# Batch 1 in a fused attention and MoE kernel: v pooled on GpSimd, weight sums on VectorE, scores in two groups, half of q transposed later

## The chip, the core and the metric

The kernel runs on one core of a Trainium2 chip. Its engines are named as the profile names them: PE (TensorE, matrix products), ACT (ScalarE, functions of one input), DVE (VectorE), POOL (GpSimd) and SP (which only issues transfers here). Each engine works through its own list of instructions in order; a wait in the list holds up all that stands behind it on that engine. The metric is the time of one execution on the device in microseconds, as the median of three runs.

## The reference

Two stages. The first is attention over pooled keys: for each of 8 batches and 8 heads, k and v (576 rows of 64) are averaged over groups of 8 rows, which leaves 72 pooled rows; then

```python
scores = scale * np.matmul(q, k_p.transpose(0, 1, 3, 2))
attn = np.exp(scores - max)          # per row
attn = attn / np.sum(attn)           # per row
attn_out = np.matmul(attn, v_p)      # 576 x 64 per head
```

The second is a network over the 4608 x 512 matrix x that the heads make side by side: `h = x @ w_in` (512 to 2048), `g = h * cos(h)`, `out = g @ w_out` (2048 to 512). The output is float32.

## The kernel before

The 4608 rows of x are worked in nine tiles of 512 rows (t = 0 to 8). For each tile there is an *up* stage (x times w_in in eight blocks, `up_mm`, line 353; then cos on ACT, line 363, and the product on DVE, line 367, into `g_sb`) and a *down* stage. Attention of batch t + 1 is done beside tile t, and since a batch has 576 rows and a tile 512, 64 rows of batch t (called REST) are left for tile t's down stage. All matrix work is in bfloat16. The order on each engine is that in which the program is written (a manual schedule): what is written earlier stands earlier in the engine's list.

Tile 0 is different from the others. Its down stage is a plain product: 64 matmuls with a 512-wide right side (`down_mm`, line 370), numbered n = 0 to 63. They run in two halves of 32; within a half the four parts of w_out are taken in the order 0, 2, 1, 3, four matmuls for each of two row blocks. A list called `fill` says before which n other work is put: batch 1's `scores`, the pooling of its v, and its `values`. From tile 1 on the down stage uses seven half-size products instead of eight, which needs sums and differences of the parts of w_out (`put_weights`, line 387: for each of two halves i four arrays w1, w3, w2, w4, in this order of dependence) and of g (`put_g`, line 397). The eight weight arrays are made once, in tile 0.

For a group of heads and columns `scores` is a matrix product into a bank of PSUM (line 233) and an exponential on ACT (line 240) that writes `ex` to SBUF. `values` is a product of `ex` with pooled v (line 268), then logarithm and exponential on ACT for the inverse of the row sum (lines 274 and 275), then two products on DVE into `xT` (line 279). For batch 1 the groups are four, `us[0]` to `us[3]`: two column ranges of 256 for heads 0 to 3, then the same for heads 4 to 7. Heads 0 to 3 need the first half of the transposed q, heads 4 to 7 the second. There are three PSUM banks of double size (`banks`) and two single ones (`obanks`); the up stage of tile 0 uses the three in turn, and the down stage its obanks.

Pooling is done in one of two ways. Batches 0 and 1 are pooled by PE, as a product with a matrix of ones and zeros (`pool_k_mm`, line 177; `pool_v_mm`, line 185, with a copy to `vz` on DVE, line 187). Batches 2 and up are loaded in a layout with one pooled row per partition, and POOL adds the eight rows in three steps (`pool_first`, line 156, four instructions; `pool_rest`, line 162, two, then line 165 for k or 168 for v).

q is transposed by PE for batches 0 and 1 (`q_transpose_mm`, line 214, in 18 blocks of 128, with copies out of PSUM at line 215) and by transfers for the others. All input loads are issued by POOL in the order of the program, and share one queue; the issue of a load waits until the load eight before it has landed. `kv_st` has two buffers, one for each of two batches or for k and v of one.

What is in the loads' order ahead of tile 0: w_in parts, batch 1's k, the two halves of its q, w_out part 0, batch 1's v, w_out parts 2, 1, 3. After tile 0 in the program, and so behind on POOL, stand the loads of batch 2 and four of the weight sums, and then the pooling of batch 2.

Of the kernel before, what the change touches and what calls it, by code (L numbers as in the profile page):

```python
# [12 lines left out]
ADD = mybir.AluOpType.add  # L13
SUB = mybir.AluOpType.subtract

POOL = 8
# [4 lines left out]
def kernel(  # L21
# [9 lines left out]
    nc = tc.nc  # L31
    B, H, S, D = q.shape
    Sp = S // POOL
# [61 lines left out]
    def load_even(dst, b, src, j0=0, j1=KCH):  # L95
        nc.gpsimd.dma_start(out=dst[:, j0:j1].rearrange("p j t d -> p j (t d)"), in_=even_view(src, b, j0, j1))

    def kv_tile():
        return kvst.tile([128, 2 * KCH * ROW * D], BF16, name="kv_st", tag="kv_st")
# [5 lines left out]
    def kv_even_tiles(b):  # L105
        st = kv_tile()
        staged["k", b], staged["v", b] = even_part(st, 0), even_part(st, 1)
# [1 line left out]
    def q_tile(b):  # L109
        staged["q", b] = qst.tile([128, KCH, ROW, D], BF16, name="q_b", tag="q_b")  # L110

    def load_kv(b, which, src):

        st = kv_tile()[:Sp, 0:H * POOL * D].rearrange("p (h t d) -> p h t d", h=H, t=POOL)
        nc.gpsimd.dma_start(out=st.rearrange("p h t d -> p h (t d)"),
                            in_=src[b].rearrange("h (p t) d -> p h (t d)", t=POOL))
        staged[which, b] = st

    def load_q(b):
        q_tile(b)  # L120
        load_even(staged["q", b], b, q)
# [6 lines left out]
    def load_w_out(cg):  # L128
        nc.gpsimd.dma_start(
            out=w_out_sb[cg],  # L130
            in_=moe_w_out[cg * 512:(cg + 1) * 512, :].rearrange("(f p) m -> p f m", p=128))
# [19 lines left out]

    def pool_first(b, which):

        x, s = staged.pop((which, b)), half_sums
        for h in range(0, H, 2):
            nc.gpsimd.tensor_tensor(out=s[:, h:h + 2], in0=x[:, h:h + 2, 0:4, :], in1=x[:, h:h + 2, 4:8, :], op=ADD)  # L156

    def pool_rest(b, which):

# [345 lines left out]
    half_pi = consts.tile([128, 1], FP32, name="half_pi")  # L505
    nc.vector.memset(half_pi, math.pi / 2.0)

    kv_even_tiles(1)
    q_tile(1)
    for cg in range(3):  # L510
        load_w_in(cg)
    load_even(staged["k", 1], 1, k)
    load_even(staged["q", 1], 1, q, 0, 2)
    load_w_in(3)
    load_even(staged["q", 1], 1, q, 2, 4)
    load_w_out(0)
    load_even(staged["v", 1], 1, v)
    nc.gpsimd.memset(vz[1], float(POOL))
    for i in range(2):
        nc.gpsimd.memset(ring[i], 0.0)  # L520
    for cg in (2, 1, 3):
        load_w_out(cg)

    def warm_up(n, bank):

# [35 lines left out]
    for t in range(NT):  # L561
        b = t + 1
        if t > 0:

            for fp in up_order(t)[0:2]:
                up_mm(t, fp, 0, 2)
        for n, fp in enumerate(up_order(t)):
            up_mm(t, fp, 2 if n < 2 else 0)
            between = ()
            if t == 0:  # L570
                if fp == 4:
                    puts = pool_k_mm(1, obanks[0], 0, 2), pool_k_mm(1, obanks[1], 2, 4)
                elif fp in (5, 6):
                    g0 = 9 * (fp - 5)
                    puts = q_transpose_mm(1, obanks[0], g0, g0 + 5), q_transpose_mm(1, obanks[1], g0 + 5, g0 + 9)
                if fp in (4, 5, 6):
                    puts[0](vec)
                    between = ((puts[1], act),)
            up_g(t, fp, between)
            if 0 < t and 3 <= n < 6:  # L580
                put_gs(*[(k, 0) for k in (((3,), (1,), ()) if t == 1 else ((1, 2), (3,), (4,)))[n - 3]])
            if 0 < t and b < B:
                if n == 0:
                    q_transpose(b)
                    k_transpose(b)
                elif n == 2:
                    pool_rest(b, "v")
                    if b + 1 < B:
                        nc.gpsimd.tensor_copy(out=gate, in_=kk[b % 2][0:1, H - 1, 0:1])
                        load_q(b + 1)  # L590
                        load_kv(b + 1, "v", v)
            if n == 2:
                while stores:
                    stores.pop(0)()
        mms = [(ms, fc) for ms in range(4) for fc in range(FFCH)]
        if t == 0:
            mms = [(ms, fc) for hm in range(2) for cg in (0, 2, 1, 3) for ms in range(2 * hm, 2 * hm + 2)
                   for fc in range(4 * cg, 4 * cg + 4)]


        def S_(n, bank):
            return lambda: scores(b, us[n], banks[bank])

        later = []

        def V_(n, bank, wait=None):
            return lambda: values(b, us[n], banks[bank], wait)

        fill = []
        if t < B:  # L610
            exp_tables()
            fill = [(1, lambda: scores(t, REST, banks[2])), (16, lambda: values(t, REST, banks[1]))]
        if t == 0:
            fill = [(2, fill[0][1]), (2, S_(0, 0)), (8, lambda: pool_v_mm(1, banks[1])),
                    (8, lambda: values(t, REST, banks[2])), (8, S_(1, 0)), (8, V_(0, 1)),
                    (18, S_(2, 2)), (21, V_(1, 0, later)), (26, S_(3, 1)), (32, lambda: later.pop()()),
                    (32, V_(2, 2)), (40, V_(3, 0))]
        if t == FIRST:
            early_inverses.clear()
        if t < FIRST:  # L620
            fi = 0
            for n, (ms, fc) in enumerate(mms):
                while fi < len(fill) and fill[fi][0] <= n:
                    fill[fi][1]()
                    fi += 1
                down_mm(obanks[ms % 2], ms, fc)
                if fc == FFCH - 1:
                    down_out(t, ms, obanks[ms % 2])
                if n == 4:
                    put_weights(0, nc.vector, (1,))  # L630
                elif n == 36:
                    put_weights(1, nc.vector, (3,))
            put_weights(1, nc.vector, (2, 4))
        else:
            products, reads = down_products(t)

            def product(i, j=0, k=2 * HF):
                for mm in products[i][j:k]:
                    mm()

            later = []

            u0, u1, u2, u3 = [(b, CHUNKS[i], banks[j]) for i, j in enumerate((2, 1, 0, 1))]
            ur = (t, REST, banks[2])

            def scores_of(*parts):
                for part in parts:
                    scores_mm(*part)
                for part in parts:
                    scores_exp(*part)  # L650

            def muls():
                while later:
                    later.pop(0)()

            steady, rest = b < B, t < B
            if rest:
                exp_tables()
            product(0)
            product(1, 0, 2)  # L660
            if steady:
                scores_of(u0, u1, u2)
            elif rest:
                scores_of(ur)
            product(1, 2)
            if t == 1:
                put_g(2, 0)
            put_gs((1, 1), (2, 1))
            reads[0]()
            if not steady:  # L670
                reads[1]()
            put_gs((3, 1), (4, 1))
            if steady:
                reads[1]()
                values_rows(*u0)
            if t == 1:
                put_g(4, 0)
            product(2)
            reads[2]()
            if steady:  # L680
                values_rows(*u1)
                values_rows(*u2)
            product(3)
            reads[3]()
            muls()
            product(4)
            reads[4]()
            muls()
            if steady:
                scores_of(ur, u3)  # L690
            product(5, 0, 4)
            if rest:
                values(*ur, later)
            product(5, 4, 12)
            muls()
            if steady:
                values_rows(*u3)
            product(5, 12)
            reads[5]()
            muls()  # L700
            product(6)
            reads[6]()
        if t < B:
            sin_tables()
        if b + 1 < B:
            if t == 0:
                load_kv(b + 1, "k", k)
                load_q(b + 1)
                load_kv(b + 1, "v", v)
                put_weights(0, nc.gpsimd, (3, 2, 4))  # L710
                put_weights(1, nc.gpsimd, (1,))
            else:

                nc.gpsimd.tensor_copy(out=gate, in_=g4[0:1, HF - 1, 0:1])  # L714
            pool_first(b + 1, "k")
            if t != 1 and b + 2 < B:
                load_kv(b + 2, "k", k)
            pool_rest(b + 1, "k")
            if t == 1:
                load_kv(b + 2, "k", k)  # L720
            pool_first(b + 1, "v")
# [28 lines left out]
```

The softmax here doesn't subtract the row's maximum and nothing guards it: scores larger than these inputs give would overflow.

## Time and profile before

| | |
|---|---|
| time | 286.22 us median of 3 (285.98 to 286.24) |
| span of the profiled run | 284.8 us |
| PE busy | 276.2 us |
| DVE busy | 215.3 us |
| ACT busy | 164.4 us |
| POOL busy | 143.4 us |
| clock of PE | full speed throughout |
| up stage of tile 0 | 17.35 to 33.59 us |
| down stage of tile 0 | 33.59 to 53.20 us |
| tile 1 | 53.20 to 83.0 us |

Times in views are in microseconds from the start of the span. In the timeline a line gives start, length, engine, line of the kernel, operation, output and inputs with their shapes, and in brackets how long the engine had been idle and who released it. In the chain a line gives start, length and what was being waited for or worked on, followed back from the last instruction. "PEld" is the loading of PE's stationary side, which overlaps its products. A share of busy time is an average over stages; what a change is worth in one stage is read from that stage.

### The profile page before, as it was taken

To read this page: it belongs to the slowest core of one execution; us is meant where nothing else is said; L and a number is where in the kernel's file an instruction comes from. 1 tells how busy PE (TensorE), PEld (TensorE's weight loads), DVE (VectorE), ACT (ScalarE), POOL (GpSimd) and SP (SyncE) were. 2 spreads that over 40 slices of the span, in tenths; PEclk is the share of its full clock that TensorE was granted. 3 is DMA by queue.
4 is the path that set the end of the run, shared out by engine and by line. 5 is a ranking of instruction groups with operands and counts; after the bars stand their busy time and mean duration, and the time that the engine had idled before them with its cause. 6 is when DMAs were issued, how large, how long until landed. Compare 5 with 4: busy or idle time off the path is not lost.

```text
span 284.8 us, 5857 instructions
## 1 busy us (share of the span) xinstructions
PE 276.2 (97%) x2360; PEld 176.4 (62%) x2360; DVE 215.3 (76%) x314; ACT 164.4 (58%) x193; POOL 143.4 (50%) x150
## 2 busy tenths in 40 slices
PE   7889999999999999999999999999999999999994
PEld 2545554446874587458745884588458844874583
DVE  5448757899957995699569956995699569856972
ACT  3787798367257735674567556655656555436600
POOL 8553069996599259924993499439900000000000
PEclk9999999999999999999999999999999999999999
DMA  7999999793939698998678969882670261015014
GB/s 154 202 206 207 207 205 216 118 199 54 145 48 161 124 221 135 138 166 169 104 135 152 186 90 160 146 172 57 119 153 3 55 128 40 0 24 126 2 37 111
DMA packets 57738, 36.12 MB, mean 127 GB/s; under 512 B 35441, under 2 KB 53361, under 8 KB 57713
## 3 DMA queue, kind: packets, MB, share of 16 engines
q0 software_dynamic: 19744, 18.07, 41.1%
q1 hardware_dynamic: 37328, 17.18, 30.0%
q10 hardware_dynamic: 640, 0.52, 0.8%
q8 instruction: 18, 0.29, 0.4%
q14 instruction: 8, 0.06, 0.1%
HBM read 36.70 MB, written 9.44 MB: 162 GB/s over the span
## 4 chain that ended last, share of the span: by engine, by line
PE 86%; DVE 6%; ACT 3%; DMA 2%; issue 1%; POOL 0%; DVEq 0%; POOLq 0%; ACTq 0%
PE bank L353 35%; PE obank L431 32%; PE obank L370 4%; PE obank L353 4%; PE bank L233 3%; DVE g_sb L367 3%; DMA q_b<-in_q_dram 2%; PE bank L295 2%; PE bank L431 2%; PE bank L268 1%; DVE w L387 1%; DVE g L397 1%; ACT cos L363 1%; ACT ex L240 1%; DVE vz L187 0%
## 5 line engine op out<-in xcount | busy, mean ns | idle before, releaser
L353 PE MATMUL bank<-xT,w_in_sb 128*128 128x512 bf16 x512 | 114.0, 379 | 0.2 <-DVE g_sb L367 0.2
L363 ACT ACTIVATE cos<-bank,half_pi 128x1024 f32<-128x1024 f32 x64 | 70.4, 1114 | 56.9 <-PE bank L353 55.0
L353 PEld LDWEIGHTS <-w_in_sb 128*128 128x128 bf16 x576 | 56.1, 98 | 66.2 <-issue 0.9
L367 DVE TENSOR_TENSOR g_sb<-bank,cos 128x1024 bf16<-128x1024 f32 x64 | 77.1, 1219 | 25.1 <-ACT cos L363 24.9
L156 POOL TENSOR_TENSOR half_sums<-kv_st 72x512 f32<-72x512 bf16 x48 | 54.7, 1165 | 0.6 <-issue 0.2
L240 ACT ACTIVATE ex<-bank 72x1024 bf16<-72x1024 f32 (+1 forms) x40 | 35.0, 929 | 34.0 <-PE bank L233 33.8
L431 PEld LDWEIGHTS <-g 128*128 128x128 bf16 x512 | 47.9, 98 | 6.1 <-issue 0.3
L431 PE MATMUL obank<-w,g 128*128 128x256 bf16 x368 | 42.7, 272 | 0.2 <-DVE p_sb L445 0.2
L431 PEld LDWEIGHTS <-g_sb 128*128 128x128 bf16 x384 | 36.8, 98 | 6.9 <-DVE g_sb L367 0.3
L162 POOL TENSOR_TENSOR half_sums<-half_sums 72x512 f32<-72x512 f32 x24 | 30.4, 1288 | 0.0
L431 PE MATMUL obank<-w_out_sb,g_sb 128*128 128x256 bf16 x240 | 28.9, 273 | 0.0
L397 DVE TENSOR_TENSOR g<-g_sb 128x1024 bf16<-128x1024 bf16 x32 | 23.3, 728 | 0.5
L714 POOL COPY gate<-g 1x1 bf16<-1x1 bf16 x5 | 0.9, 179 | 34.1 <-DVE g L397 34.1
L279 DVE TENSOR_TENSOR xT<-bank,inv 64x256 bf16<-64x256 f32 x14 | 5.9, 422 | 15.0 <-ACT inv L275 14.9
L300 DVE TENSOR_TENSOR x_rows<-bank,inv_rows 128x512 bf16<-128x512 f32 x24 | 16.6, 691 | 0.8
L431 PE MATMUL obank<-w_out_sb,g 128*128 128x256 bf16 x112 | 15.6, 273 | 0.0
L431 PE MATMUL obank<-w,g_sb 128*128 128x256 bf16 x128 | 15.3, 273 | 0.0
L370 PE MATMUL obank<-w_out_sb,g_sb 128*128 128x512 bf16 x64 | 15.2, 379 | 0.0
L353 PE MATMUL obank<-xT,w_in_sb 128*128 128x512 bf16 x64 | 15.1, 379 | 0.0
L233 PE MATMUL bank<-qT,kk 64*72 64x128 bf16 (+2 forms) x288 | 12.7, 221 | 0.1
L233 PEld LDWEIGHTS <-kk 64*72 64x72 bf16 x288 | 8.8, 110 | 5.3 <-issue 3.8
L331 ACT ACT_TABLE_LOAD x9 | 11.5, 1283 | 0.9 <-PEq L734 0.7
(103 smaller groups left out, 277.1 us busy)
## 6 DMA issues: line engine op xcount, KB each, us to landing
out_dram<-o_two SPq DMA_DIRECT2D x64, 128.0 KB, 2.4
kv_st<-in_v_dram POOLq DMA_DIRECT2D x8, 576.0 KB, 11.2
kv_st<-in_k_dram POOLq DMA_DIRECT2D x7, 576.0 KB, 8.5
q_b<-in_q_dram POOLq DMA_DIRECT2D x6, 576.0 KB, 7.5
w_in_sb<-in_moe_w_in_dram POOLq DMA_DIRECT2D x4, 512.0 KB, 13.5
w_out_sb<-in_moe_w_out_dram POOLq DMA_DIRECT2D x4, 512.0 KB, 18.2
q_b<-in_q_dram POOLq DMA_DIRECT2D x4, 288.0 KB, 12.4
g_sb<-in_k_dram SPq DMA_DIRECT2D x1, 576.0 KB, 3.6
```

The source lines that it names most:

```text
L156: nc.gpsimd.tensor_tensor(out=s[:, h:h + 2], in0=x[:, h:h + 2, 0:4, :], in1=x[:, h:h + 2, 4:8, :], op=ADD)
L162: add(out=s[:, h:h + 4, 0:2, :], in0=s[:, h:h + 4, 0:2, :], in1=s[:, h:h + 4, 2:4, :], op=ADD)
L233: nc.tensor.matmul(pair[:Sp, bank, c:c + n].rearrange("p (g n) -> p g n", n=64), lhsT=kk[b % 2][half[r], key_slot(b, h0 + i, r), 0:Sp], rh ...
L240: nc.scalar.activation(out=ex[:, 0:nh * n].rearrange("p (a n) -> p a n", a=2), in_=pair[:Sp, :, 0:nh * n // 2], func=ACTF.Exp, scale=scale ...
L300: nc.vector.tensor_tensor(out=x[0:n].rearrange("p (j a d) -> p j a d", j=KCH, a=2), in0=ps[0:n, :, 0:2 * (D + 2)].rearrange("p j (a w) -> ...
L331: nc.scalar.preload_act_table_set("natural_log_exp_and_others")
L353: nc.tensor.matmul(h[j] if h is obanks else h[:, j, :], lhsT=w_in_sb[fc // 4][:, ki, (fc % 4) * 128:(fc % 4 + 1) * 128], rhs=xT[:, ki, t * ...
L363: nc.scalar.activation(out=c, in_=ps, func=ACTF.Sin, bias=half_pi[:, :1])
L367: nc.vector.tensor_mul(out=o, in0=ps, in1=c)
L370: nc.tensor.matmul(o, lhsT=g_sb[:, fc, ms * 128:(ms + 1) * 128], rhs=w_out_sb[fc // 4][:, fc % 4, :], start=(fc == 0), stop=(fc == FFCH - 1))
L397: nc.vector.tensor_tensor(out=out[:, f0:f1], in0=x, in1=y, op=op)
L431: mms.append(lambda bank=bank, first=first, g=g, w=w, fc=fc, p=p: nc.tensor.matmul(bank[p], lhsT=g(fc, p), rhs=w(fc), start=(first and fc ...
```

## The change

Five edits, all for batch 1 and tile 0.

1. Batch 1's v is loaded in the layout with pooled rows on partitions, in two parts of four heads (one into the second half of batch 1's `kv_st`, one into `g1`, which isn't used until tile 1), and pooled by POOL ahead of tile 0. `pool_v_mm(1, ...)` goes. This is to take that product from PE.
2. The loads' order becomes: w_out 0, v, w_out 2, the second half of q, w_out 1, w_out 3, and batch 2's k and q are issued ahead of the pooling of v.
3. The four weight sums that POOL did are put on DVE: w1 of half 0 after the sixth up block, the others at n = 24 of the down stage.
4. The second half of batch 1's q is transposed at n = 15 of the down stage, with both copies on DVE, instead of in the up stage with one copy on ACT.
5. Scores are put in two groups, REST with `us[0]` and `us[1]` at n = 8, `us[2]` with `us[3]` at n = 16; values of the first three groups stand together at n = 24, and their products on DVE are put off to n = 32.

```diff
-    def load_kv(b, which, src):
-        st = kv_tile()[:Sp, 0:H * POOL * D].rearrange("p (h t d) -> p h t d", h=H, t=POOL)
-        nc.gpsimd.dma_start(out=st.rearrange("p h t d -> p h (t d)"),
-                            in_=src[b].rearrange("h (p t) d -> p h (t d)", t=POOL))
-        staged[which, b] = st
+    def load_kv(b, which, src, homes=None):
+        homes = homes or [kv_tile()]
+        n = H // len(homes)
+        staged[which, b] = []
+        for i, home in enumerate(homes):
+            st = home[:Sp, 0:n * POOL * D].rearrange("p (h t d) -> p h t d", h=n, t=POOL)
+            nc.gpsimd.dma_start(out=st.rearrange("p h t d -> p h (t d)"),
+                                in_=src[b, i * n:(i + 1) * n].rearrange("h (p t) d -> p h (t d)", t=POOL))
+            staged[which, b] += [st[:, h:h + 2] for h in range(0, n, 2)]
...
-    load_even(staged["q", 1], 1, q, 2, 4)
     load_w_out(0)
-    load_even(staged["v", 1], 1, v)
+    load_kv(1, "v", v, [st[:, KCH * ROW * D:], g1.rearrange("p f n -> p (f n)")])
     nc.gpsimd.memset(vz[1], float(POOL))
     for i in range(2):
         nc.gpsimd.memset(ring[i], 0.0)
-    for cg in (2, 1, 3):
+    load_w_out(2)
+    load_even(staged["q", 1], 1, q, 2, 4)
+    for cg in (1, 3):
         load_w_out(cg)
+    load_kv(2, "k", k)
+    load_q(2)
+    pool_first(1, "v")
+    pool_rest(1, "v")
...
-                elif fp in (5, 6):
-                    g0 = 9 * (fp - 5)
-                    puts = q_transpose_mm(1, obanks[0], g0, g0 + 5), q_transpose_mm(1, obanks[1], g0 + 5, g0 + 9)
+                elif fp == 5:
+                    puts = q_transpose_mm(1, obanks[0], 0, 5), q_transpose_mm(1, obanks[1], 5, 9)
...
+            if t == 0 and fp == 5:
+                put_weights(0, nc.vector, (1,))
...
+        def late_q():
+            for put in [q_transpose_mm(1, banks[0][:, i, :], g0, g1) for i, g0, g1 in ((0, 9, 14), (1, 14, 18))]:
+                put(vec)
...
-            fill = [(2, fill[0][1]), (2, S_(0, 0)), (8, lambda: pool_v_mm(1, banks[1])),
-                    (8, lambda: values(t, REST, banks[2])), (8, S_(1, 0)), (8, V_(0, 1)),
-                    (18, S_(2, 2)), (21, V_(1, 0, later)), (26, S_(3, 1)), (32, lambda: later.pop()()),
-                    (32, V_(2, 2)), (40, V_(3, 0))]
+            fill = [(8, lambda: scores_of((t, REST, banks[2]), (b, us[0], banks[0]), (b, us[1], banks[1]))),
+                    (11, lambda: values(t, REST, banks[2], later)), (15, late_q),
+                    (16, lambda: scores_of((b, us[2], banks[0]), (b, us[3], banks[1]))), (16, muls),
+                    (24, V_(0, 2, later)), (24, V_(1, 0, later)), (24, V_(2, 1, later)),
+                    (24, lambda: put_weights(0, nc.vector, (3, 2, 4))), (24, lambda: put_weights(1, nc.vector, (1,))),
+                    (32, muls), (44, V_(3, 2))]
...
-                if n == 4:
-                    put_weights(0, nc.vector, (1,))
-                elif n == 36:
+                if n == 36:
                     put_weights(1, nc.vector, (3,))
...
-                load_kv(b + 1, "k", k)
-                load_q(b + 1)
                 load_kv(b + 1, "v", v)
-                put_weights(0, nc.gpsimd, (3, 2, 4))
-                put_weights(1, nc.gpsimd, (1,))
```

`scores_of` and `muls`, which existed for the later tiles, are moved up so that tile 0 can use them.

## The prediction

> **What bounds the kernel now.** First the page: busy times, to see which engine could set the end. Then the busy time by stage, then inside the odd stages the chain and the timeline.
>
> ```profile
> PE 276.2 (97%) x2360; PEld 176.4 (62%) x2360; DVE 215.3 (76%) x314; ACT 164.4 (58%) x193; POOL 143.4 (50%) x150
> ```
>
> TensorE (PE) is busy 97% of the span. What doesn't shorten PE's work or its few waits can't pay. By stage (columns: stretch, length, then busy time and instructions of PE, PEld, DVE, ACT, POOL, then clock, DMA share, GB/s): the up and the down matmul of tile 0, all of tile 1, all of tile 2.
>
> ```profile
> 17.35:33.59 16.24, 16.24 (x156) 8.42 (x155) 11.64 (x15) 11.69 (x16) 5.40 (x8) 1.00 1.23 207
> 33.59:53.20 19.61, 19.32 (x131) 9.52 (x130) 12.05 (x18) 16.34 (x23) 15.03 (x10) 1.00 1.10 195
> 53.20:83.00 29.80, 29.34 (x258) 19.52 (x257) 26.94 (x36) 17.05 (x19) 24.48 (x24) 1.00 0.73 118
> 83.14:112.16 29.02, 29.00 (x257) 19.30 (x256) 23.17 (x35) 17.05 (x19) 19.94 (x21) 1.00 0.95 151
> ```
>
> Tile 2 is full of PE (29.00 of 29.02 us), and the later steady tiles are like it. Tile 1 has the same work and takes 0.8 us more. All edits lie before or in tile 0's down matmul, so only the first three rows can change. The chain in the down stage and at its end:
>
> ```profile
> 36.22 1.19 PE bank L185 x18
> ...
> 37.50 0.70 DVE vz L187
> 38.20 0.05 issue
> 38.24 0.61 PE bank L268 x4
> ...
> 53.40 0.69 DVE o_two L375
> 54.09 2.21 DVE w L387
> 56.30 0.02 issue
> 56.32 1.65 DVE w L387
> 57.97 1.15 DVE g_sb L367
> ```
>
> Two things to see. Batch 1's v is pooled by PE (1.19 us), and its first values wait for the copy out of PSUM. And from 53.40 on the chain runs on VectorE (DVE): two weight sums take 3.9 us and hold back the first cos products of tile 1. Why they take so long is in the timeline of POOL (GpSimd) and DVE:
>
> ```profile
> 36.08 0.68 DVE L387 TENSOR_TENSOR w<-w_out_sb 128x1024 bf16<-128x1024 bf16 x1
> 53.23 2.50 POOL L162 TENSOR_TENSOR half_sums<-half_sums 72x512 f32<-72x512 f32 x2
> 54.01 2.28 DVE L387 TENSOR_TENSOR w<-w,w_out_sb 128x1024 bf16<-128x1024 bf16 x1
> 55.81 2.34 POOL L165 TENSOR_TENSOR ring<-half_sums 72x512 bf16<-72x512 f32 x2
> 56.32 1.65 DVE L387 TENSOR_TENSOR w<-w_out_sb,w 128x1024 bf16<-128x1024 bf16 x1
> ```
>
> The same sum is 0.68 us with POOL at rest, and 2.28 and 1.65 us beside POOL's adds: the first ends just after L162's pair does (55.73).
>
> [...]
>
> **The change, part by part.**
>
> *v pooled on POOL.* Removed from PE: 18 matmuls, 1.17 us of pure path, and DVE's copy (0.69 us) with the wait behind it. Added on POOL: four first adds of 1.15, two of 1.25, one of 1.27 us = 8.4 us, in place of the four weight sums there (4 x 2.13 = 8.5 us). What matters is when it ends. Landing times before, as issue plus time to landing: w_in's last part 27.8, q second half 29.3, w_out 0 31.8, v 34.7, w_out 2 37.2, w_out 1 40.0, w_out 3 42.4, k of batch 2 46.5 us; all in one queue at some 206 GB/s. In the new order w_out 0 lands at 30.4 (2.55 us a part), the two halves of v at 31.9 and 33.4 (1.45 each), w_out 2 at 36.0, q at 37.4; then w_out 1, w_out 3 and k as before, since the bytes ahead of them are the same. POOL then pools v from 32 to about 40.7 us. The first values stand at down matmul 24, which PE reaches at about 41.8: hidden, with 1 us to spare.
>
> *The second half of q's transposes moved into the down matmul.* Nine transposes, 0.50 us by the chain, leave the up stage and come back in the down stage: no change in work. What is new is a wait. They stand at matmul 15, their two copies are both on DVE (0.49 and 0.41 us), and only one down matmul (0.22 us) stands between them and the scores that read the result and reuse that bank. From the end of the transposes to the end of the second copy is about 0.9 us, so PE waits 0.7 us. Behind it on PE is everything; this is the largest new cost. Bounds: 0.4 if the first copy overlaps the transposes fully, 1.0 if DVE is late.
>
> *Scores in two groups.* The first group stands at matmul 8 and needs all three banks, the last being free only when the last cos product is done (ACT ends 1.3 us after the up stage, DVE 1.25 later): at about 35.7 us, where PE would be there at 35.4. Wait: 0.3 us. In exchange the old waits go: the stage of before holds 64 down matmuls (24 of them take 5.20 us on the chain, so 64 x 0.217 = 13.9), pooling 1.2, 16 scores in fours at 0.34 (1.4), 16 values in fours at 0.44 (1.8), the small ones of batch 0 some 0.4: 18.6 of 19.61 us, so 1.0 us was waiting or switching (the v copy, and values that waited for a bank, 0.53 us before 47.57 among them). In the new order ACT has an exponential per group done before PE asks for it: values of groups 0 to 2 stand together at 24, with the exponentials done at about 41.9 and w_out 3 landed at 42.4.
>
> *Weight sums on DVE.* One at 31.7 in the gap left by a q copy (w_out 0 landed at 30.4, so no wait in front of the cos product behind it). Four more at about 40.3 to 43.1, 0.69 each, when POOL has just finished pooling and waits for k (46.5): no blocking, and they end before the first output copy at 44.2. If v were late they would meet POOL's adds and cost 1.6 to 2.3 us each; then the output copies, and PE's second half behind them, come 1 to 4 us later. That is the upper bound of this edit.
>
> *Sum up to tile 1.* Up stage 16.24 - 0.5 = 15.7. Down stage: work 18.6 - 1.2 + 0.5 = 17.9; waits 0.7 (q), 0.3 (banks), 0 to 0.3 (w_out 2 at matmul 8, wanted at 36.0 and landing at 36.0), 0.1 (output copy): 19.0 to 19.3. Together 34.7 to 35.0 against 35.85: PE reaches tile 1 some 0.8 to 1.1 us earlier.
>
> *Tile 1.* Its start hangs on DVE's last two weight sums, which will again meet POOL. POOL pools k of batch 2 as soon as it lands, 46.5 instead of 47.14 (where it was held by its own weight sums): L162 and L165 come 0.65 us earlier. DVE arrives at the sums at about 53.5, in the middle of L162 again, and leaves 0.65 to 0.9 us earlier than 57.97. The gain that survives is the smaller: 0.65 to 0.9; I take 0.8.
>
> Forecast: 286.2 - 0.8 = 285.4 us.
>
> **The rivals.**
>
> *A: the new waits eat the gain.* The loads are just in time: w_out 2 and q are wanted within 0.5 us of landing. If v in its new shape (72 partitions) moves as slowly as k of batch 2 did (42.4 to 46.5, 4.1 us instead of 2.9), all behind it is 1.2 us later, PE waits that long at matmul 8, and 0.8 - 1.2 makes 286.6; with part of it, 286.2. Against: stores began at 45.3, in that same stretch, and the bandwidth stayed at 206 GB/s, so k wasn't slow but shared.
>
> *B: DVE becomes the bound; slower.* Pooling of v ends late (43 or after), the four weight sums run into it and take 1.7 us each, +4 us on DVE, half of it absorbed before the second half of the down matmul: 286.2 + 1.2 = 287.4. For: DVE is already the chain at the tile's border. Against: POOL has about 8 us between v's landing and the time that it is wanted, and little else to do.
>
> *C: more is won.* If DVE's last two sums fall beside POOL's work rather than into it (0.7 each instead of 2.2 and 1.65), tile 1 loses its 0.8 us too: 285.4 - 1.0 = 284.4. Against: k's landing, which starts POOL's adds, doesn't move.
>
> **How the numbers follow.** Forecast 55%, A 22%, B 13%, C 10%. The forecast's own bounds are 285.0 (all waits at their lower ends) to 285.8 (0.4 us more wait on w_out 2); the range takes in C's 284.4 and A's upper end, 286.8, and leaves out B. Faster by over 0.2% means under 285.65: most of the forecast (48 of 55) and C: 0.58. Within 0.2% (285.65 to 286.79): the rest of the forecast and most of A (18 of 22): 0.25. Slower: B and the end of A: 0.17.
>
> **What the profile of the changed kernel would show.** Right: no pooling of v on PE; PE's wait before the second group of scores, 0.7 us, released by DVE's q copies; vz written by POOL before 41.8 us; the four weight sums at 0.7 us each; the last two still at 1.6 to 2.3 beside L162 and L165; tile 1 begun by PE at about 52.3 instead of 53.2, and from tile 2 on 28.95 us a tile. Wrong: down matmuls waiting for a w_out part or for q's load (A), weight sums of 1.6 us or more near 41 us or output copies released late (B), or tile 1 down at 29.0 us (C). The prediction fails most easily on the load order, since every load there is wanted within a microsecond of landing.

## The result, and the profile after

The changed kernel takes 295.5 us (median of 4 runs, 295.02 to 298.52) against 286.23 us before in the same comparison (4 runs, 285.98 to 286.74): 1.034 times as long, with a 95% interval of 1.028 to 1.040. Forecast were 285.4 us, and a range up to 286.8. The prediction is wrong in sign, and off by 10 us.

In the changed kernel nearly every line number is 3 higher than before: the weight sums are L390, `put_g` is L400, POOL's first adds are L159, the next L165, the last L168 (k) and L171 (v), down matmuls L373, the products of later tiles L434. First the page of the changed kernel: busy times, and the clock granted to PE in 40 slices of 7.3 us.

```profile
PE 277.1 (94%) x2342; PEld 176.9 (60%) x2342; DVE 222.8 (76%) x318; ACT 164.0 (56%) x192; POOL 143.5 (49%) x154
...
PEclk9999999999959999999999999999999999999998
```

PE has no more to do than before (277.1 to 276.2 us), but 3 points less of the span: the time is idle time. DVE gained 7.5 us. And one slice of the clock stands out, the twelfth, from 81 to 88 us. The same stretches as in the prediction say where (length, then busy time of PE, PEld, DVE, ACT, POOL, then clock, DMA share, GB/s):

```profile
17.35:33.59 16.24, 16.24 (x149) 8.14 (x148) 11.75 (x15) 11.54 (x15) 7.59 (x11) 1.00 1.24 206
33.59:53.20 19.61, 16.99 (x117) 8.88 (x115) 12.80 (x20) 15.87 (x23) 12.55 (x12) 1.00 1.16 198
53.20:83.00 29.80, 24.07 (x183) 14.55 (x182) 29.24 (x30) 13.08 (x13) 24.70 (x24) 0.96 0.70 108
83.14:112.16 29.02, 28.76 (x235) 18.32 (x234) 21.40 (x32) 17.03 (x19) 11.87 (x14) 0.93 0.81 137
```

The up stage of tile 0 is as full as before. In the down stage's stretch PE idles 2.6 us (before 0.3), in tile 1's stretch 5.7 (before 0.5). DVE is busy 29.24 of 29.80 us there (before 26.94), which looks like more work; 6.39 us of it are one blocked instruction, as the timeline below shows. By PE's first matmul of each stage, tile 0 takes 36.7 us (before 35.8), tile 1 37.7 (before 29.8), and all that follows 0.4 us more than before; PE began 0.3 us earlier. Together 0.9 + 7.9 + 0.4 - 0.3 = 8.9 us; the profiled spans differ by 8.8. PE's waits between 17 and 95 us (total, times, longest):

```profile
PE obank L434 <- DVE v_sb L450: 5.4, 1, 5.4
PE obank L373 <- DMA w_out_sb<-in_moe_w_out_dram: 1.6, 2, 0.8
PE bank L236 <- DVE qT L218: 0.8, 1, 0.8
```

The first is the large loss. The timeline of the changed kernel about it:

```profile
72.98 1.91 PE L434 MATMUL obank<-w,g 128*128 128x256 bf16 x16 [0.23 <-DVE p_sb L448]
74.41 4.47 POOL L159 TENSOR_TENSOR half_sums<-kv_st 72x512 f32<-72x512 bf16 x4
75.48 6.39 DVE L400 TENSOR_TENSOR g<-g_sb,g 128x1024 bf16<-128x1024 bf16 x1
78.85 2.47 POOL L165 TENSOR_TENSOR half_sums<-half_sums 72x512 f32<-72x512 f32 x2
81.80 0.68 DVE L450 TENSOR_TENSOR v_sb<-obank,p_sb 128x512 f32<-128x512 f32 x1
82.53 3.57 PE L434 MATMUL obank<-w,g 128*128 128x256 bf16 x16 [5.40 <-DVE v_sb L450]
```

And the same place in the kernel before:

```profile
73.84 0.18 POOL L714 COPY gate<-g 1x1 bf16<-1x1 bf16 x1 [4.76 <-DVE g L397]
74.24 1.15 POOL L156 TENSOR_TENSOR half_sums<-kv_st 72x512 f32<-72x512 bf16 x1 [0.23 <-issue]
75.06 0.87 DVE L397 TENSOR_TENSOR g<-g_sb,g 128x1024 bf16<-128x1024 bf16 x1
75.36 1.58 POOL L156 TENSOR_TENSOR half_sums<-kv_st 72x512 f32<-72x512 bf16 x1
```

It is one sum, `put_g(4, 0)`, which the program puts in tile 1 behind the point where POOL is released to pool batch 3's k. Both times it comes to DVE during POOL's first add. Before, it got in when that add ended, and the *second* add was held back (1.58 instead of 1.15 us). After, it came 0.07 us ahead of the first add's end, stayed out until the sixth add had ended (81.32), and took 6.39 us instead of 0.68. Behind it on DVE stands the operation that frees PE's bank (L450), so PE waits 5.40 us. Then PE's next 16 matmuls take 3.57 us where 16 of the same form took 1.91 (72.98): the granted clock is 0.50 from 82.5 to 86.1 us, as the twelfth slice above shows. No edit of the change touches this sum, this gate or these adds.

### The profile page after: what moved, and what is told of

Its sections match the earlier page's. It is cut to its first block, busy times and chain, and to the rows that moved or that the text cites. A ratio compares the mean times of both kernels' runs of the same rounds, so it can differ in the third digit from the quotient of the medians.

```text
span 293.6 us, 5829 instructions
## 1 busy us (share of the span) xinstructions
PE 277.1 (94%) x2342; PEld 176.9 (60%) x2342; DVE 222.8 (76%) x318; ACT 164.0 (56%) x192; POOL 143.5 (49%) x154
## 3 DMA queue, kind: packets, MB, share of 16 engines
q1 hardware_dynamic: 37328, 17.18, 30.4%
## 4 chain that ended last, share of the span: by engine, by line
PE 64%; DVE 3%; DMA 2%; ACT 0%; issue 0%
PE obank L434 27%; PE bank L356 27%; PE obank L356 4%; PE bank L236 2%; DMA xT<-x_rows 2%; DVE g_sb L370 2%; PE bank L434 2%; PE bank L298 2%; DVE g L400 1%; PE bank L271 1%; ACT cos L366 0%; DVE o_two L450 0%
## 5 line engine op out<-in xcount | busy, mean ns | idle before, releaser
L159 POOL TENSOR_TENSOR half_sums<-kv_st 72x512 f32<-72x512 bf16 x50 | 56.1, 1148 | 8.0 <-DMA kv_st<-in_k_dram 6.7
L434 PEld LDWEIGHTS <-g 128*128 128x128 bf16 x512 | 48.7, 99 | 12.5 <-issue 6.1
L434 PE MATMUL obank<-w,g 128*128 128x256 bf16 x368 | 44.5, 279 | 5.6 <-DVE v_sb L450 5.4
L434 PEld LDWEIGHTS <-g_sb 128*128 128x128 bf16 x384 | 36.8, 98 | 7.2 <-DVE g_sb L370 0.5
L165 POOL TENSOR_TENSOR half_sums<-half_sums 72x512 f32<-72x512 f32 x26 | 32.9, 1285 | 0.1
L434 PE MATMUL obank<-w_out_sb,g_sb 128*128 128x256 bf16 x240 | 28.9, 273 | 0.3 <-DVE g_sb L370 0.3
L400 DVE TENSOR_TENSOR g<-g_sb 128x1024 bf16<-128x1024 bf16 x32 | 23.7, 740 | 0.5
L400 DVE TENSOR_TENSOR g<-g_sb,g 128x1024 bf16<-128x1024 bf16 x16 | 16.6, 1038 | 0.0
L373 PE MATMUL obank<-w_out_sb,g_sb 128*128 128x512 bf16 x64 | 15.0, 379 | 1.6 <-DMA w_out_sb<-in_moe_w_out_dram 1.6
L434 PE MATMUL obank<-w_out_sb,g 128*128 128x256 bf16 x112 | 15.8, 275 | 0.0
L434 PE MATMUL obank<-w,g_sb 128*128 128x256 bf16 x128 | 15.3, 273 | 0.0
## 6 DMA issues: line engine op xcount, KB each, us to landing
q_b<-in_q_dram POOLq DMA_DIRECT2D x4, 288.0 KB, 12.1
```

What stands on the lines that cost most here:

```text
L159: nc.gpsimd.tensor_tensor(out=half_sums[:, 2 * i:2 * i + 2], in0=x[:, :, 0:4, :], in1=x[:, :, 4:8, :], op=ADD)
L165: add(out=s[:, h:h + 4, 0:2, :], in0=s[:, h:h + 4, 0:2, :], in1=s[:, h:h + 4, 2:4, :], op=ADD)
L373: nc.tensor.matmul(o, lhsT=g_sb[:, fc, ms * 128:(ms + 1) * 128], rhs=w_out_sb[fc // 4][:, fc % 4, :], start=(fc == 0), stop=(fc == FFCH - 1))
L400: nc.vector.tensor_tensor(out=out[:, f0:f1], in0=x, in1=y, op=op)
L434: mms.append(lambda bank=bank, first=first, g=g, w=w, fc=fc, p=p: nc.tensor.matmul(bank[p], lhsT=g(fc, p), rhs=w(fc), start=(first and fc ...
```

## The experiments

Two theories stood against each other. **T1**: the sum is shut out by POOL's run as a whole, and the loss is that meeting; what made it harmless before was something small. **T2**: the loss lies in the edits themselves (late loads, weight sums on DVE), and the long sum is only where it surfaces. Ratios are against the kernel before on the same chip, with 95% intervals; where none is given, the time is that of one execution.

### The meeting taken away, the edits kept

The changed kernel with the gate in front of the pooling of batch 3's k moved behind the sum:

```diff
-                nc.gpsimd.tensor_copy(out=gate, in_=g4[0:1, HF - 1, 0:1])
+                nc.gpsimd.tensor_copy(out=gate, in_=g4[0:1, (3 if t == 1 else HF - 1), 0:1])
```

By T1 the sum then takes 0.7 us instead of 6.4, PE's wait of 5.4 us goes, and the time falls to 286.4 to 287.2 us.

> The changed kernel, with the one-element copy that gates GpSimd's pooling in tile 1 reading the last-made part of g4, so that GpSimd starts after VectorE's put_g(4, 0), not beside it. [...] Rival (the new load order and the later start of tile 1 upset the transposes and loads of tile 1, and VectorE's long sum is only where that shows): 293 us or more.

Measured: 289.96 us, ratio 1.011 (1.007 to 1.015). The sum took 0.68 us, the wait of 5.4 us was gone, and tile 1 took 30.8 us. So 5.5 of the 9.3 us came back, which rules out the rival, but the rest, 3.7 us, was more than T1 had allowed (0.2 to 1.0). At the start of tile 1 the last two weight sums met POOL's adds in full (2.58 and 1.65 us). And the later gate has a price of its own: the run began 3.3 us later than in the changed kernel, and in tile 2 sums of g met POOL (1.64 us at 94.63, where 0.7 is usual).

### Is it the instant at which the sum arrives?

Before, the sum had arrived 0.3 us ahead of the end of an add. A filler on DVE ahead of it shifts the arrival: in the kernel before by 0.4 us, in the changed kernel by 0.9, counted from the start of POOL's first add.

```diff
+                nc.vector.memset(pad, 0.5)     # 128 x 432 (before), 128 x 864 (after)
                 put_g(4, 0)
```

> The kernel before, with one 128x432 memset (about 0.45 us) on VectorE ahead of put_g(4, 0) in tile 1; nothing else of the change. Theory that the arrival time of the sum against GpSimd's adds decides: it now comes just after an add has begun, as in the changed kernel, and is shut out for several adds: 290 to 295 us. Rival (the other edits are the cause, the sum gets in at the next end of an add): 286.4 to 287.4 us.

> The changed kernel, with one 128x864 memset (about 0.9 us) on VectorE ahead of put_g(4, 0) in tile 1, so that the sum comes some 0.3 us before the end of an add, as in the kernel before. If the arrival within an add decides, the sum gets in at the next end, and the time is 287 to 289 us although VectorE has more to do. If only the first end of a run of adds lets VectorE in, the sum is shut out to the same point, 81.3 us, and the time stays 294 to 296 us.

Measured: 286.6 and 297.02 us. The timeline of the kernel before with the filler:

```profile
75.20 1.78 POOL L156 TENSOR_TENSOR half_sums<-kv_st 72x512 f32<-72x512 bf16 x1
75.35 0.63 DVE L397 TENSOR_TENSOR g<-g_sb,g 128x1024 bf16<-128x1024 bf16 x1
```

and of the changed kernel with it:

```profile
77.62 5.48 DVE L400 TENSOR_TENSOR g<-g_sb,g 128x1024 bf16<-128x1024 bf16 x1
77.87 1.14 POOL L159 TENSOR_TENSOR half_sums<-kv_st 72x512 f32<-72x512 bf16 x1
```

In the first the sum came *after* the recorded start of the second add and still got in at once; in the second it came 0.3 us ahead of an add's end, as in the kernel before, and was shut out until POOL's run ended (82.6; the sum ended at 83.1). Each is one execution, but they go against the idea in both directions: the instant within an add doesn't decide.

### A gap made in POOL's run

The changed kernel, with each first add of that pooling followed at once by the add that needs its result, so that POOL has to wait between them:

```diff
-            pool_first(b + 1, "k")
+            if t == 1:
...
+                for i, x in enumerate(staged.pop(("k", b + 1))):
+                    h = slice(2 * i, 2 * i + 2)
+                    add(out=s[:, h], in0=x[:, :, 0:4, :], in1=x[:, :, 4:8, :], op=ADD)
+                    add(out=s[:, h, 0:2, :], in0=s[:, h, 0:2, :], in1=s[:, h, 2:4, :], op=ADD)
...
```

By T1, with a pause between two adds the sum waits for one add at most, 0.7 to 1.9 us instead of 6.4, and the time is 287.5 to 290 us.

> The changed kernel, with GpSimd's pooling of batch 3's k in tile 1 reordered so that each add of four rows is followed at once by the add that needs its result (eight instructions that each wait for the one before, in place of six that follow without a break). [...] Rival (GpSimd has priority over VectorE, pause or none): put_g(4, 0) still takes 5 us or more and the time stays at 294 us or more.

Measured: 292.39 us. In this kernel's timeline the sum meets the first add as before and gets in at its end:

```profile
74.17 1.14 POOL L728 TENSOR_TENSOR half_sums<-kv_st 72x512 f32<-72x512 bf16 x1
75.24 0.68 DVE L400 TENSOR_TENSOR g<-g_sb,g 128x1024 bf16<-128x1024 bf16 x1
75.39 1.13 POOL L729 TENSOR_TENSOR half_sums<-half_sums 72x256 f32<-72x256 f32 x1
```

Tile 1 took 29.3 us and tile 2 began at 83.1, as in the kernel before. So a pause in POOL's run, here 0.08 us in which the next add waits for a result, was enough. The time was missed all the same. Tile 0 took 1.0 us more than in the kernel before, tile 2 3.3 us more, and tile 3 1.7. At the end of tile 2 PE waited 2.62 us for the transposes of x (until 115.38 us), and its next 24 matmuls took 7.03 us instead of 5.34, at half clock from 116.6 to 120.0. Ahead of that, one transpose of q (84.9 us) took 8.69 us instead of 6.39, and the loads of q and v behind it were issued 2 us later than before (98.0 and 98.8 instead of 96.0 and 96.8). That this makes the transposes of x late is read from these times; no run isolates it.

### Where did the pause before come from?

The kernel before has a pause of 0.23 us in front of its run, with no releaser ("issue" in its lines above), and a block of 8 KB came at 75.4 us on q14, one of the two queues that the profile gives the kind "instruction". In the changed kernel such a block came at 64.9 and none on that queue from 66 to 77, and there was no pause. If the pause is POOL waiting for its next instructions, which was the author's estimate from these times, then a few more instructions ahead should move its place. So: the kernel *before*, with four one-element writes on POOL at 19 us and nothing else.

```diff
     for i in range(2):
         nc.gpsimd.memset(ring[i], 0.0)
+    for i in range(4):
+        nc.gpsimd.memset(gate, 0.0)
```

> The kernel before, with four one-element memsets added to GpSimd's list at about 19 us, where it is idle; nothing else. In the kernel before, GpSimd's run of adds in tile 1 begins with a pause of 0.23 us put down to instruction issue, and an instruction fetch lands at 75.4 us; in the changed kernel there is neither. Theory (this pause is what let VectorE's put_g(4, 0) in; the place of the pause in GpSimd's list moves by four instructions, away from that run): put_g(4, 0) is shut out and takes 5 us or more, and the time is 292 to 296 us. Rival (something in the change itself shuts VectorE out, not the place of a fetch): 286.0 to 286.8 us.

Measured: 295.51 us, the changed kernel's time. Its timeline:

```profile
74.82 1.15 POOL L156 TENSOR_TENSOR half_sums<-kv_st 72x512 f32<-72x512 bf16 x1
75.90 6.39 DVE L397 TENSOR_TENSOR g<-g_sb,g 128x1024 bf16<-128x1024 bf16 x1
75.94 1.14 POOL L156 TENSOR_TENSOR half_sums<-kv_st 72x512 f32<-72x512 bf16 x1
```

Such a block came at 64.9 us, the 0.23 us pause was gone, the sum took 6.39 us, PE waited 5.4, and tile 1 took 37.8 us. Tile 0 was unchanged (35.8). This decides for T1: four instructions of no use, without a single edit of the change, make the same wait and cost 9 us.

If the meeting is the whole cost, then putting the sum ahead of the gate must give it all back, in this shifted kernel:

```diff
-            put_gs((3, 1), (4, 1))
+            put_gs(*(((3, 1), (4, 0), (4, 1)) if t == 1 else ((3, 1), (4, 1))))
...
-            if t == 1:
-                put_g(4, 0)
```

> The kernel before with the four one-element POOL memsets that alone made it 295.5 us, and with put_g(4, 0) put ahead of put_g(4, 1), so that no sum of DVE stands behind the gate when POOL's pooling of batch 3's k begins. If the sum shut out by POOL's unbroken run is the whole of the 9 us: put_g(4, 0) takes 0.7 us, PE has no wait over 1 us in tile 1, tile 1 takes 29.5 to 30.5 us instead of 37.8, the clock stays at full speed, and the time is 286 to 287.5. If the shift does harm in other places too: over 288.

Measured: 286.81 us, ratio 1.002 (1.001 to 1.003). The sum takes 0.68 us, and POOL's adds run unbroken behind it with nothing to meet:

```profile
73.49 0.68 DVE L397 TENSOR_TENSOR g<-g_sb,g 128x1024 bf16<-128x1024 bf16 x1
74.45 4.49 POOL L156 TENSOR_TENSOR half_sums<-kv_st 72x512 f32<-72x512 bf16 x4
```

No wait of PE in tile 1 is over 0.3 us, and tile 1 took 29.9 us. 8.7 of the 9.2 us came back. (The profiled execution, of 288.11 us, is one of the longer of the twenty: its tile 2 took 30.4 us, with two waits of 0.6 and 0.5 us at the end.)

### What the edits themselves cost

The same new order in the changed kernel:

> The changed kernel, but in tile 1 the weight sum put_g(4, 0) stands ahead of put_g(4, 1), so ahead of the gate that releases POOL's pooling of batch 3's k. Theory (all of the large loss is this one sum shut out by POOL's unbroken run): the sum takes 0.68 us, PE's wait of 5.4 us and the slow clock after it go, tile 1 takes 29.3 to 30.7 us instead of 37.7, and the time is 286.8 to 290: what remains over 286.2 is tile 0 (0.5 to 0.9 us longer than before) and sums of later tiles that fall beside POOL's adds anew. Rival (the pooling is still in the way, of another instruction): another sum or copy of DVE takes 3 us or more in tile 1 or 2 and the time stays over 291.

Measured: 289.28 us, ratio 1.008 (1.006 to 1.010). Tile 1 took 29.5 us, so the rest of the loss is in tile 0 (36.4), in tile 2 (30.7, of which 1.55 is one wait at its end) and 0.4 us in tile 4. In tile 0 PE waited 0.71 and 0.59 us for parts 2 and 3 of w_out. Two kernels, both on top of this one, ask why those are late. In one, batch 2's k and q are issued behind the pooling of v:

```diff
-    load_kv(2, "k", k)
-    load_q(2)
     pool_first(1, "v")
     pool_rest(1, "v")
+    load_kv(2, "k", k)
+    load_q(2)
```

> As the run before it, but POOL issues the loads of batch 2's k and q after it has pooled batch 1's v, at about 40.5 us instead of 28.3. If k, queued early, takes bandwidth from w_out's last parts, w_out 3 lands at 42.4 to 43 instead of 44.55, PE's wait of 0.85 us for it goes, and k still lands by 48. If it is the two 72-partition halves of v that cost the time (2.0 us each instead of 1.45), w_out 3 lands at 44.5 again and k lands at 48 or later. Time 286.5 to 289 in the first case, 287.5 to 290 in the second.

In the other, v is loaded whole at the same place of the queue, and pooled by PE as before the change:

```diff
-    load_kv(1, "v", v, [st[:, KCH * ROW * D:], g1.rearrange("p f n -> p (f n)")])
+    staged["v", 1] = even_part(st, 1)
+    load_even(staged["v", 1], 1, v)
...
-    pool_first(1, "v")
-    pool_rest(1, "v")
...
+                    (18, lambda: pool_v_mm(1, banks[2])),
```

> The changed kernel with put_g(4, 0) ahead of the gate as in the first of these runs, and with batch 1's v loaded whole on 128 partitions, at the same place of the queue, and pooled on PE again (18 matmuls, 1.2 us, at down matmul 18). If the halves of v are what made the loads late: w_out 3 lands at about 42.5 and batch 2's k at about 46.5, PE's waits for w_out 2 and 3 (1.6 us together) go, tile 0 takes 35.5 to 36.3 us in spite of the 1.2 us more on PE (after 36.7), and the time is 285.8 to 288. If the loads are late for another reason (k queued early, the new order): w_out 3 still lands at 44 or after, tile 0 takes 37.5 us or more, and the time is 288 to 291.

Measured: 290.03 us (ratio 1.012, 1.010 to 1.014) with the loads issued later, and 286.92 us (1.0024, 1.0001 to 1.0047) with v whole. With the later issue w_out 3 landed at 43.5 us, between the two cases expected, and the time is over both ranges. PE's wait for w_out 3 went (that for w_out 2, 0.69 us, stayed), but k of batch 2 landed at 47.7 and the border sums met POOL in full (2.38 and 1.64 us): what tile 0 gained (35.8 us), tile 1 lost (31.1). With v whole, w_out 3 landed at 41.9 and k at 45.7, in a profile that stands 0.5 us earlier as a whole: that is 2.1 and 1.7 us sooner than in the changed kernel. Both waits for w_out went, and tile 0 took 36.1 us although PE pools v again.

A profile can stand earlier or later as a whole (here by 0.5 us), so the landing of w_out 0, which none of these edits moves, is the better mark. From it to the landing of w_out 3 it took 14.0 us in the kernel with the sum first, 13.4 with the later issue, and 12.1 with v whole, where k is issued early too (the bytes between the two landings would take 11.9 us at 206 GB/s). So v in two parts of 72 partitions is most of the lateness; the early issue of k adds 0.5 us beside the two parts, and nothing to be seen without them. Against the run with its two parts, v back on PE is worth 2.4 us. By the profiles only 0.3 us of that lie in tile 0; 1.2 lie in tile 2 and 0.4 in tile 4, and no run says why.

One wait of the change was left in that kernel: the late transposes of q. Two down matmuls more between them and their scores:

```diff
-                    (11, lambda: values(t, REST, banks[2], later)), (15, late_q),
+                    (11, lambda: values(t, REST, banks[2], later)), (13, late_q),
```

> The version with v on PE and put_g(4, 0) ahead of the gate (286.92 us), with the late q transposes at down matmul 13 instead of 15, so that three down matmuls (0.65 us) stand between them and the scores that read them. If the step that gave this wait to the two copies on DVE is right, PE's wait there falls from 0.77 to 0.2 to 0.4 us, tile 0 gets as much shorter, and the time is 286.2 to 286.6: level with the kernel before. If the wait only moves elsewhere in tile 0 (the load of q, a bank), the time stays at 286.8 to 287.

Measured: 286.56 us, ratio 1.0014 (0.9994 to 1.0034). PE's wait for the q copies, in this kernel's timeline:

```profile
39.37 0.63 PE L236 MATMUL bank<-qT,kk 64*72 64x256 bf16 x8 [0.34 <-DVE qT L218]
```

0.34 instead of 0.77 us, as expected, and tile 0 took 35.9. This is the best form of the change that was found. Its median is level with the kernel before and not better, and it scatters more: 5 of its 22 executions took 288.0 to 289.9 us, where 1 of 43 of the kernel before took over 287.2.

### The sums at the border, in the kernel before

The prediction's rival C held that tile 1 would be shorter if the last two weight sums were free of POOL. POOL's second adds for batch 2's k were put behind the last of these sums (and one write of zeros at the start given to DVE, so that POOL's list kept its length):

```diff
+            if t == 0:
+                nc.gpsimd.tensor_copy(out=gate, in_=w4[1][0:1, 3, 0:1])
```

> The kernel before, with GpSimd's second and third adds for batch 2's k held back (by a one-element copy) until VectorE's last weight sum is done, and one memset moved from GpSimd to VectorE to keep GpSimd's list as long as it was. The two last weight sums should take 0.7 us each instead of 2.3 and 1.65, and the first cos product of tile 1 starts when its input is there: 285.6 to 286.0 us if the later adds don't meet VectorE more often and the pause in GpSimd's list stays where it was; 292 us or more if the pause moves off the run in tile 1.

and the same with `put_g(4, 0)` ahead of the gate in tile 1:

> As the one before, and in tile 1 put_g(4, 0) is put ahead of put_g(4, 1), so that GpSimd's run, which is gated on put_g(4, 1), can't meet it. Theory: no sum of more than 2 us on VectorE wherever the pause in GpSimd's list lies, and 285.4 to 286.2 us. If this is slower than 286.6 us, then the order of the sums or the later start of GpSimd costs more than the overlap did.

Measured: 286.81 us (ratio 1.0007, 0.9996 to 1.0019) and 287.05 us (1.0023, 1.0007 to 1.0039). Both are above what was expected. The two sums fell to 0.7 us, but POOL then ran later and met two sums of g (in the first kernel 1.69 us at 62.22 and 1.73 at 64.96), where it had met one (1.81 us at 62.68). Tile 1 took 29.9 and 30.1 us, no less than before (29.8): what the border gained went to the later meetings.

## Why the prediction was wrong

**The failed step: "Tile 1".** The prediction took tile 1 to change only at its start, by weight sums that "will again meet POOL", and bounded a blocked sum at 1.6 to 2.3 us. Two things are wrong in that. The bound: it took the longest sum at the border, 2.28 us, for the most that a meeting costs, although that very sum had waited for more than one add: it came at 54.01 us, during the first add of L162's pair, which ended at 54.51, and got in only behind the second. In the changed kernel the sum stayed out to the end of the sixth, 6.39 us: here the wait reached over the whole row of adds that followed one another without a pause. And the place: tile 1's timeline of before showed a sum of two SBUF inputs (75.06 us) inside a run of POOL's adds, with the second add stretched to 1.58 us. That it got in there hung on the place of something in POOL's list, which four more instructions moved; a pause of 0.23 us marks the place. The step didn't ask which other meetings there were, nor whether they would stay as cheap. The cost is 5.40 us of wait, 1.66 us on the 16 slow matmuls, and 0.5 us on the 20 behind them (0.88 and 0.82 us for groups that took 0.56 and 0.61 before): 7.6 of the 7.9 us by which tile 1 grew.

**"Down stage" was too short by 1.7 to 2 us.** It claimed 1.0 us of waits and switching to be had in the old stage, from 18.6 us of work added up from groups. The prediction's own second row said otherwise: PE was busy 19.32 of 19.61 us. The 0.53 us before 47.57 that it counted among the waits is one of PE's weight loads (PEld); PE itself stood still for 0.04 us there. After, the stage takes 21.0 us. PE is idle for 2.6 (forecast 1.1 to 1.4) and busy for 18.3, near to 19.3 - 1.2 + 0.5 = 18.6 and not at 17.9.

**The load order, called the weakest point, was weak by its size.** The halves of v took 1.9 and 2.0 us to land and not 1.45, a figure worked out from bytes alone at 206 GB/s. So v landed at 32.1 and 34.1 (forecast 31.9 and 33.4), w_out 2 at 36.55 (36.0), q at 38.0 (37.4), w_out 3 at 44.55 (42.4), k of batch 2 at 47.9 (46.5). The timeline of PE in the changed kernel has the two waits, and the forecast one for q:

```profile
36.60 0.81 PE L373 MATMUL obank<-w_out_sb,g_sb 128*128 128x512 bf16 x3 [0.75 <-DMA w_out_sb<-in_moe_w_out_dram]
39.99 0.63 PE L236 MATMUL bank<-qT,kk 64*72 64x256 bf16 x8 [0.77 <-DVE qT L218]
44.61 4.56 PE L373 MATMUL obank<-w_out_sb,g_sb 128*128 128x512 bf16 x20 [0.85 <-DMA w_out_sb<-in_moe_w_out_dram]
```

This is rival A, and it is true as far as it goes: tile 0 became 0.9 us longer instead of 0.8 to 1.1 shorter. The forecast left nothing for it beyond 0.3 us. Its argument against A was that the bandwidth had stayed at 206 GB/s beside k of batch 2. The runs show that this says little: while the two halves of v landed (30.2 to 34.1 us) the DMA moved 204 GB/s, some 0.8 MB where the halves are 0.59, so other bytes moved beside them and the halves came late at the same rate. With v whole the same bytes took 2.8 us (29.8 to 32.6) at 207 GB/s.

**What was right.** PE's pooling of v went. The wait for the q copies was 0.77 us (0.7), that for the bank 0.26 (0.3). POOL had v at 40.48 us (40.7). The four weight sums that came from POOL (2.12 to 2.14 us each there before, 38.55 to 47.18 us) met nobody (DVE's own first one, at n = 4 before, only moved up to the sixth up block), on DVE's timeline:

```profile
40.86 0.69 DVE L390 TENSOR_TENSOR w<-w_out_sb,w_out_sb 128x1024 bf16<-128x1024 bf16 x1
...
42.92 0.68 DVE L390 TENSOR_TENSOR w<-w_out_sb 128x1024 bf16<-128x1024 bf16 x1
```

so rival B fell. The last two weight sums were still held, 1.02 and 1.65 us, and the first cos product of tile 1 began at 58.3 us (before 57.9): no earlier, since k landed later, not earlier. From tile 2 on tiles take 28.9 us but for one of 29.4. Rival C named 284.4 us; in the two kernels at the border free sums brought nothing, since POOL's adds met other sums instead.

**What stays open.** That the 0.23 us pause is POOL waiting for its instructions rests on three things: it has no releaser, a block comes on q14 one to two us behind it (75.4 us before, 75.2 with the filler), and four more instructions ahead move both away. Against it: in the two kernels with v on PE a block came at 74.7 and 75.6 us with no such pause to be seen. Nor is it shown how the pause lets the sum in: it stands in front of the first add, and the sum got in behind that add, 1.1 us later. The two go together in all six kernels where the sum stands behind the gate and the adds are not broken up: in the three with the pause it got in at once, in the three without it it was shut out to the end of the run.

And a run without a pause doesn't always shut DVE out. In the kernel before, a weight sum at 49.15 us took 0.80 us between two of POOL's first adds of k, and the next add took 1.59; in tile 1 a sum of g got in between two of POOL's adds of v (1.81 us at 62.68, and the next add took 1.72 instead of 1.26; in the changed kernel 1.81 us at 63.10). What tells these from the sum at 75.48 us is open. So is the wait of 1.55 us at the end of tile 2 in the changed kernel with the new order.

## What to carry to other kernels

List every VectorE sum of two SBUF tiles that can be live while GpSimd works through several adds in a row, and price each at the whole run (here 6.39 us for a sum of 0.68), not at one instruction, since these runs don't say which meetings end early; then put it ahead of the gate that releases the run. That a meeting is cheap in the profile before is no safety where it hangs on a pause of 0.23 us: four instructions more on that engine moved it here. Where a stage's row already shows its bounding engine at 98% busy (here 19.32 of 19.61 us), hardly any wait is left to be won there, and loads that land within 1 us of their use should be priced by a measured transfer of the same shape, since the rate of the DMA doesn't say that the first load in the queue lands on time (here w_out 3 landed at 44.55 us and not at 42.4, while 204 GB/s moved beside the halves of v).

## What the runs showed of the hardware that was not expected

- Four one-element writes on GpSimd, 55 us ahead, made a kernel of 286.2 us one of 295.5.
- A VectorE sum of 0.68 us was shut out to the end of six GpSimd adds back to back (6.39 us, and 5.48 where it came later), and got in after one where the next add had to wait 0.08 us for a result. Other sums got in between adds with no pause to be seen (0.80 us at 49.15, before).
- After 5.4 us without work PE's next 16 matmuls took 3.57 us instead of 1.91, 1.9 times as long, at a granted clock of 0.50. In the kernel with gaps half clock for 3.4 us followed a wait of 2.62 us, and 24 matmuls took 7.03 us instead of 5.34 (that run's mean granted clock is 0.994). So a wait of PE can cost more than its length, here 5.4 + 2.2 and 2.6 + 1.7.
- Two loads of 288 KB on 72 partitions took 3.9 us to land, one of 576 KB on 128 partitions at the same place of the queue 2.8 us, while the DMA moved 204 and 207 GB/s: the late landing doesn't show in the rate.
